# Two f32 products of raw tiles in the first block, and the first logit sum of four block pairs moved behind the up-weights

## The chip, the cores and the metric

The kernel runs on one core of one Trainium2 chip. The metric is the device time of one execution in microseconds (us). The core's engines each run their own instruction stream in order and wait for each other by semaphores: TensorE (PE, with its weight loads listed apart as PEld), VectorE (DVE), ScalarE (ACT), GpSimd (POOL) and SyncE (SP). In this kernel SP and POOL issue nearly all the transfers (DMAs).

## What is computed

```python
x = A_x                                              # 1 x 2048 x 640, f32
g = sigmoid((x * gate_w).sum(-1, keepdims=True))     # one gate for each of the 2048 positions
a = Re(DFT_seq(DFT_hidden(x)))                       # four f32 matrix products by cosine and sine tables
b = (gelu(x @ w_gate) * (x @ w_up)) @ w_down         # w_gate, w_up: 640 x 1728
return g * a + (1 - g) * b
```

All operands are f32. The sum `x * gate_w` that stands under the sigmoid is called the logit sum below; there are 16 of them, each for 128 positions.

## The kernel before

**Products in parts.** An f32 operand is split in a high part (ACT rounds it to the type fp32r, `high`, L82) and a low part (DVE subtracts the high part from the raw tile, `low`, L85). `mm3` (L101 to L103) makes a product of three fp32r matmuls: high by high, high by low, low by high. A matmul of a raw f32 tile without parts appears nowhere in this kernel.

**The first block.** The hidden width 1728 is 13 blocks of 128 and a rest of 64. The "mixed" block holds the 64 left columns of the gate and of the up matrix side by side; it is made first, along with gate block 0 and up block 0, in the banks `pm`, `pg` and `pu`, for the first two of four position tiles (512 positions each). The depth 640 is five steps `d` of 128. The part of the program from L1019 on is written out by hand in the order in which ACT, DVE and PE take it: PE first makes 14 matmuls of ones (`idle`, L1023) that need no load. Then step d = 0 of `pm` is made in two halves of 256 positions with three fp32r matmuls each (L1051), so that the first half can start when half of the x tile is there. `pg` and `pu` follow with `mm3` on all 512 columns, then the same three for the second position tile, `x012`. The raw tiles are `w0r` (weights) and `xr` (x), with `w0h`, `w0l`, `x011h`, `x011l` and so on as their parts. A number in a tile's name that is not part of the tile's own name is left out by the profile, so every raw x tile reads `xr`.

**The pairs of blocks.** Blocks 1 and 2 are made one by one, and the other ten in five pairs, f and f + 1, for f = 3, 5, 7, 9 and 11. A pair's first block makes seven extra products across position tiles for the gate (banks such as `pH5t`, `pZ5t`) and seven for the up matrix (`pH5u`, `pZ5u`). The latter need the up-weights' sums and differences: raw tile `wu5r`, four DVE instructions (L246 to L249, `across`), the high part `wu5h` on ACT and the low part `wu5l` on DVE. They also need parts of x sums that were stored earlier and are loaded again by POOL: `xu` (three loads, `load_across`, L1150), and `xq` for the gate.

**What sets the order.** `fills` is a queue of small pieces of DVE and ACT work with a cost each. While PE's products are written out, `fill` takes pieces from its head in step with the cost of the products, so that the order in `fills` is the order on DVE, with the PE-driven instructions in between. In pairs 5, 7, 9 and 11 (`kind == 1 and f > PAIRED`) two logit sums are put in: `load_z(2)` returns a load and a sum (L720, tile `xz`, DVE) twice. The first load goes out at once. The first sum `z1` and the second load stand in the middle of `fills` (`len(fills) // 2`), the second sum `z2` at its end, ahead of the next block's weights (`work`). When they are placed, `fills` holds nine pieces: four sums left over from the block before, the three pieces of the up-weights (`across`, `high_u`, `low_u`) and the two pieces of the down-weights' sums (L595 to L600, tiles `dr` and `da`, stored by SP as `wsd`).

**Buffers.** All tiles of 4 KB a partition share 46 slots (`slot`). A tile gets a slot when the program asks for it, and the first write to it waits for the last use of the tile that had the slot before. So the order in which tiles are asked for decides which instruction waits for which.

**POOL's transfers.** The hidden rows go to device memory through POOL (`hA`, `hT`, L404, 256 KB each), which issues them in order. A transfer of POOL waits for the transfer that was issued eight places before it, apart from its data.

Of the kernel before, what the change touches and what calls it, by code (L numbers as in the profile page):

```python
# [37 lines left out]
def kernel(  # L38
# [27 lines left out]
    nc = tc.nc  # L66
# [317 lines left out]
    def load_first():  # L384

        r, h, l = ([slot(dt, [P, 8, P], f"w0{n}{k}") for k in range(2)] for n, dt in (("r", F32), ("h", F32R), ("l", F32R)))
        W = {n: [tuple(v[c // 8][:, c % 8] for v in (h, l)) for c in range(k, 3 * ND, 3)] for k, n in enumerate("mgu")}

        def at8(v, a, b):
            return v[a // 8][:, a % 8 : a % 8 + b - a]  # L390

        def load(engine, a, b):
            engine.dma_start(at8(r, a, b), w0[:, a:b])

        def parts(do, a, b):
            if do is high:
                high(at8(h, a, b), at8(r, a, b))
            else:
                low(at8(h, a, b), at8(l, a, b), at8(r, a, b))

        return W, load, parts

    def keep(to, i, src):
        nc.gpsimd.dma_start(to[:, i], src)  # L404
# [580 lines left out]
            put(2 * q + 1, 0, a[q])  # L985


    W0, load_part, parts = load_first()
    Bs = []
    B, tiles, load, piece, tsum, his, lows = load_x(0)  # L990

# [4 lines left out]
    halves = [slice(0, T // 2), slice(T // 2, T)]  # L996
# [22 lines left out]
    with in_order(ACT, DVE, PE):  # L1019
        nc.scalar.activation(table, table, AF.Gelu_apprx_tanh)  # L1020
        idle = bank("idle")
        for k in range(14):
            nc.tensor.matmul(idle[:, halves[k % 2]], *ones, start=k == 0, stop=True, skip_group_check=True)  # L1023
        bk1, bk2 = first_banks(0, 1), first_banks(0, 2)
        for d in range(ND):
            raw, _, (h, l) = piece(d, 1)
            first, *rest = FIRST[d]
            parts(high, *first)
            if d == 0:
                a, b = halves  # L1030
                nc.vector.tensor_copy(h[:, a], raw[:, a])
                parts(low, *first)
                low(h[:, a], l[:, a], raw[:, a])
                split(h[:, b], l[:, b], raw[:, b])
                parts(high, *rest[0])
                parts(low, *rest[0])
            else:
                high(h, raw)
                parts(low, *first)
                low(h, l, raw)  # L1040
                for r in rest:
                    parts(high, *r)
                for r in rest:
                    parts(low, *r)
            split_piece(d, 2)
            if d == 0:
                wh, wl = W0["m"][0]
                for c in halves:
                    for k, (w, x) in enumerate(((wh, h), (wl, h), (wh, l))):
                        first = k == 0 and c is halves[0]  # L1050
                        nc.tensor.matmul(bk1["m"][:, c], w, x[:, c], start=first, stop=False, skip_group_check=True)  # L1051
                for n in "gu":
                    mm3(bk1[n], W0[n][0], (h, l), True, False)
            else:
                first_products(bk1, W0, B, 1, [d])
            first_products(bk2, W0, B, 2, [d])
# [121 lines left out]
    with in_order(PE, ACT, DVE, POOL):  # L1178
        for f in range(1, NF):
# [24 lines left out]
            if kind == 1 and f > PAIRED:  # L1204
                (_, first), z1, (_, second), z2 = load_z(2)
                first()
                k = len(fills) // 2
                more = list(fills)
                fills.clear()
                fills.extend([*more[:k], z1, (0, second), *more[k:], z2, *work])  # L1210
            elif f in ZE_AT:
                (_, first), z1 = load_z(1)
                first()
                fills.insert(5, z1)
# [45 lines left out]
            W = nxt  # L1260
# [438 lines left out]
```

## Time and profile before

| what | us |
|---|---|
| median of 3 runs (1020.52 to 1021.36) | 1020.55 |
| the profiled execution's own time | 1021.83 |
| its span, first to last instruction | 1020.0 |
| PE busy, 4483 matmuls | 1015.6 |
| DVE busy, 1154 instructions | 823.2 |
| ACT busy, 622 instructions | 486.1 |
| POOL busy | 166.9 |

The profiled execution took 1.8 us more than its span; a launch lies around the span. It took 1.3 us more than the median of the runs that were timed without a profile. Times of single events below are counted from the span's start. Matmuls overlap by a part of their length, so the distance between two starts, not their duration, is what one costs. A row of the timeline gives start, duration, engine, line, what is written from what, and in square brackets how long the engine sat idle before it and what released it.

### The profile page before, as it was taken

Reading aid. Unit: us, or ns where it says so; the run is one execution under the profiler, and the core shown is the slowest. Engines: PE = TensorE matmul, PEld = TensorE weight load, DVE = VectorE, ACT = ScalarE, POOL = GpSimd, SP = SyncE. Lnnn points to the kernel's source line nnn. Section 1 sums busy time; section 2 is a strip of 40 time slices with the busy share of each in tenths; the row PEclk is TensorE's granted clock in tenths of the full one; section 3 lists DMA queues with packets and bytes.
Section 4 is the critical chain, followed back from the end, with each engine's and each line's share of the span. In section 5 each row is a group of like instructions: output and inputs, shape, how many; then the busy total and the mean of one; then the engine's idle time right before and its main releaser. Section 6 shows DMA issues by size and latency. Waiting matters only on the chain.

```text
span 1020.0 us, 13269 instructions
## 1 busy us (share of the span) xinstructions
PE 1015.6 (100%) x4483; PEld 840.2 (82%) x4483; DVE 823.2 (81%) x1154; ACT 486.1 (48%) x622; POOL 166.9 (16%) x295
## 2 busy tenths in 40 slices
PE   9999999999999999999999999999999999999998
PEld 7888888888888888888888888888888888888887
DVE  6987877787787989888887976898588869797796
ACT  5544534353535667557444443444344444455440
POOL 0122242323231200100001012102210200021112
PEclk9999999999999999999999999999999999999999
DMA  7468588968699999979874669668866877897856
GB/s 271 168 209 276 181 264 275 314 225 290 201 315 313 415 374 383 330 245 329 295 254 172 213 223 337 223 200 298 302 203 209 294 252 275 295 349 215 274 134 99
DMA packets 96644, 267.58 MB, mean 262 GB/s; under 512 B 12672, under 2 KB 27008, under 8 KB 96576
## 3 DMA queue, kind: packets, MB, share of 16 engines
q1 hardware_dynamic: 70512, 185.24, 53.2%
q0 software_dynamic: 25776, 81.30, 24.4%
q8 instruction: 35, 0.57, 0.2%
q14 instruction: 33, 0.27, 0.1%
q10 hardware_dynamic: 288, 0.20, 0.1%
HBM read 192.48 MB, written 70.27 MB: 258 GB/s over the span
## 4 chain that ended last, share of the span: by engine, by line
PE 97%; issue 1%; DMA 1%; DVE 0%; POOL 0%; POOLq 0%
PE pX L103 6%; PE pX L102 6%; PE pX L101 6%; PE pZ L103 4%; PE pZ L102 4%; PE pZ L101 4%; PE pL L102 3%; PE pL L103 3%; PE pL L101 3%; PE pV L102 2%; PE pV L103 2%; PE pV L101 2%; PE pY L102 1%; PE pR L103 1%; PE pQ L101 1%; PE pQ L102 1%
## 5 line engine op out<-in xcount | busy, mean ns | idle before, releaser
L82 ACT ACTIVATE ch<-csa 128x1024 fp32r<-128x1024 f32 x32 | 34.0, 1063 | 78.2 <-DVE csa L770 76.7
L85 DVE TENSOR_TENSOR cl<-cra,ch 128x1024 fp32r<-128x1024 f32 x32 | 39.1, 1222 | 24.6 <-ACT ch L82 22.5
L82 ACT ACTIVATE ch<-cra 128x1024 fp32r<-128x1024 f32 x32 | 33.9, 1059 | 52.3 <-DVE cl L85 19.3
L85 DVE TENSOR_TENSOR cl<-crb,ch 128x1024 fp32r<-128x1024 f32 x32 | 39.1, 1223 | 14.4 <-ACT ch L82 14.4
L102 PE MATMUL pL<-cl,xah 128*128 128x512 f32 x128 | 49.9, 390 | 0.0
L103 PE MATMUL pL<-ch,xal 128*128 128x512 f32 x128 | 49.9, 390 | 0.0
L101 PE MATMUL pL<-ch,xah 128*128 128x512 f32 x128 | 49.7, 390 | 0.0
L82 ACT ACTIVATE ch<-crb 128x1024 fp32r<-128x1024 f32 x32 | 33.8, 1055 | 31.2 <-PE pL L102 11.4
L404 POOL DMA_DIRECT2D hA<-s x48 | 26.1, 544 | 132.7 <-DVE s L562 113.1
L85 DVE TENSOR_TENSOR cl<-csb,ch 128x1024 fp32r<-128x1024 f32 x32 | 39.2, 1225 | 3.7 <-ACT ch L82 2.3
L85 DVE TENSOR_TENSOR cl<-csa,ch 128x1024 fp32r<-128x1024 f32 x32 | 39.1, 1221 | 2.1 <-ACT ch L82 1.1
L82 ACT ACTIVATE ch<-csb 128x1024 fp32r<-128x1024 f32 x32 | 34.0, 1062 | 11.7 <-DVE csb L773 4.7
L556 ACT ACTIVATE s<-s 128x512 f32<-128x512 f32 x24 | 15.2, 633 | 46.7 <-DVE s L555 46.7
L148 ACT ACTIVATE s<-pX 128x512 f32<-128x512 f32 x40 | 23.5, 598 | 23.7 <-PE pX L103 22.4
L85 DVE TENSOR_TENSOR kl<-kw,kh 128x1024 fp32r<-128x1024 f32 x24 | 29.4, 1223 | 4.5 <-DMA kw<-in_wd 2.6
L82 ACT ACTIVATE kh<-kw 128x1024 fp32r<-128x1024 f32 x24 | 25.3, 1052 | 16.1 <-PE kR L103 6.2
L551 DVE TENSOR_TENSOR s<-s,pX 128x512 f32<-128x512 f32 x24 | 16.5, 686 | 19.6 <-PE pX L103 14.3
L1346 POOL DMA_DIRECT2D uA<-c x8 | 4.3, 542 | 168.9 <-DVE c L1448 168.7
L404 POOL DMA_DIRECT2D hT<-s x48 | 26.0, 541 | 24.3 <-DVE s L579 8.1
L929 POOL DMA_DIRECT2D out<-ks x12 | 6.5, 541 | 136.8 <-DVE ks L928 136.2
L101 PEld LDWEIGHTS pL<-ch,xah 128*128 128x128 f32 x128 | 24.0, 188 | 5.0
L102 PEld LDWEIGHTS pL<-cl,xah 128*128 128x128 f32 x128 | 24.0, 188 | 5.0
(3612 smaller groups left out, 3483.8 us busy)
## 6 DMA issues: line engine op xcount, KB each, us to landing
cra<-in_ct SPq DMA_DIRECT2D x64, 512.0 KB, 4.6
crb<-in_ct SPq DMA_DIRECT2D x64, 512.0 KB, 5.0
hA<-s POOLq DMA_DIRECT2D x48, 256.0 KB, 5.9
hT<-s POOLq DMA_DIRECT2D x48, 256.0 KB, 5.7
kr<-hA SPq DMA_DIRECT2D x24, 512.0 KB, 7.7
kr<-hT SPq DMA_DIRECT2D x24, 512.0 KB, 6.8
ux<-uA SPq DMA_DIRECT2D x24, 512.0 KB, 5.9
ux<-uT SPq DMA_DIRECT2D x16, 512.0 KB, 6.7
```

The source lines that it names most:

```text
L82: nc.scalar.activation(hi, raw, AF.Copy)
L85: nc.vector.tensor_tensor(lo, raw, hi.bitcast(F32), op=ALU.subtract)
L101: nc.tensor.matmul(ps, lh, rh, start=first, stop=False, skip_group_check=True)
L102: nc.tensor.matmul(ps, lh, rl, start=False, stop=False, skip_group_check=True)
L103: nc.tensor.matmul(ps, ll, rh, start=False, stop=last, skip_group_check=True)
L148: nc.scalar.activation(m, src, AF.Copy)
L404: nc.gpsimd.dma_start(to[:, i], src)
L551: tt(s5, s5, X, op=ALU.add)
L556: nc.scalar.activation(s2, s2, AF.Gelu_apprx_tanh)
L929: nc.gpsimd.dma_start(acc4[:, t] if tp and e == 4 else out[2 * tp + t, e], src)
L1346: nc.gpsimd.dma_start(to[:, i], src)
```

## The change

Three places differ.

```diff
@@ load_first
-        return W, load, parts
+        return W, r[0][:, 0], load, parts
@@ the first block
-    W0, load_part, parts = load_first()
+    W0, w0m, load_part, parts = load_first()
...
-        for k in range(14):
+        for k in range(12):
             nc.tensor.matmul(idle[:, halves[k % 2]], *ones, start=k == 0, stop=True, skip_group_check=True)
...
             if d == 0:
-                wh, wl = W0["m"][0]
                 for c in halves:
-                    for k, (w, x) in enumerate(((wh, h), (wl, h), (wh, l))):
-                        first = k == 0 and c is halves[0]
-                        nc.tensor.matmul(bk1["m"][:, c], w, x[:, c], start=first, stop=False, skip_group_check=True)
+                    first = c is halves[0]
+                    nc.tensor.matmul(bk1["m"][:, c], w0m, raw[:, c], start=first, stop=False, skip_group_check=True)
                 for n in "gu":
                     mm3(bk1[n], W0[n][0], (h, l), True, False)
@@ the pairs 5, 7, 9 and 11
                 (_, first), z1, (_, second), z2 = load_z(2)
                 first()
-                k = len(fills) // 2
+                k = len(fills) - 2
                 more = list(fills)
                 fills.clear()
                 fills.extend([*more[:k], z1, (0, second), *more[k:], z2, *work])
```

The first block's six fp32r matmuls of 256 columns become two f32 matmuls on the raw tiles, and the matmuls of ones go from 14 to 12. The parts of these tiles are still made, since `pg`, `pu` and the second position tile use them. In the pairs the first sum and the second load now stand behind seven of the nine pieces instead of four, that is behind the up-weights' `across`, `high_u` and `low_u`.

PE at the program's start, before. The `x011h` and `x011l` are parts of the first x tile, `w0h` and `w0l` of the first weights.

```order
L1023 MATMUL idle<-const-bfloat16-1.0 128x256
L1051 MATMUL pm_193<-x011h,w0h_138 128x256
L1051 MATMUL pm_193<-x011h,w0l_140 128x256
L1051 MATMUL pm_193<-x011l,w0h_138 128x256
L1051 MATMUL pm_193<-x011h,w0h_138 128x256
L1051 MATMUL pm_193<-x011h,w0l_140 128x256
L1051 MATMUL pm_193<-x011l,w0h_138 128x256
L101 MATMUL pg_194<-x011h,w0h_138 128x512
```

And in the changed kernel:

```order
L1023 MATMUL idle<-const-bfloat16-1.0 128x256
L1049 MATMUL pm_191<-xr_142,w0r_136 128x256 x2
L101 MATMUL pg_192<-x011h,w0h_138 128x512
L102 MATMUL pg_192<-x011l,w0h_138 128x512
L103 MATMUL pg_192<-x011h,w0l_140 128x512
```

The two raw products read the loaded tiles themselves and wait for their loads alone; the first instruction that waits for DVE's and ACT's parts is now `pg`'s.

DVE in pair 5, before. L720 is a logit sum (two instructions), L246 to L249 and `wu5l` belong to the up-weights, L454 to L460 read PE's banks, and L595 to L600 are the down-weights' sums.

```order
L720 ISA xz_1411,z<-xz_1411,gwb 128x640
L720 ISA z 128x1
L454 TENSOR_TENSOR s_1431<-s_1431,pH5t 128x512
L246 TENSOR_TENSOR wu5r<-wu5r 128x128
L247 TENSOR_TENSOR wu5r<-wu5r 128x128
L248 TENSOR_TENSOR wu5r<-wu5r 128x128
L249 TENSOR_TENSOR wu5r<-wu5r 128x128
L459 TENSOR_TENSOR s_1450<-s_1450,pZ5t 128x512
L460 TENSOR_TENSOR s_1450<-s_1450,pX_1_1461 128x512
L85 TENSOR_TENSOR wu5l<-wu5r,wu5h 128x640
L595 TENSOR_TENSOR dr_1407<-da_1408,dr_1407 128x256
```

And in the changed kernel:

```order
L246 TENSOR_TENSOR wu5r<-wu5r 128x128
L247 TENSOR_TENSOR wu5r<-wu5r 128x128
L248 TENSOR_TENSOR wu5r<-wu5r 128x128
L249 TENSOR_TENSOR wu5r<-wu5r 128x128
L454 TENSOR_TENSOR s_1425<-s_1425,pH5t 128x512
L459 TENSOR_TENSOR s_1444<-s_1444,pZ5t 128x512
L460 TENSOR_TENSOR s_1444<-s_1444,pX_1_1455 128x512
L85 TENSOR_TENSOR wu5l<-wu5r,wu5h 128x640
L720 ISA xz_1405,z<-xz_1405,gwb 128x640
L720 ISA z 128x1
L595 TENSOR_TENSOR dr_1401<-da_1402,dr_1401 128x256
```

The sum moved past eight instructions and stands between the low part and the down-weights' sums; pairs 7, 9 and 11 read the same.

SP in pair 5, with the semaphores that each row waits for: the two `xz` loads and the first store of the down-weights' sums. Before:

```order
L716 DMA xz_1411<-in_xz 128x640 [waits DMASW4_49,DMASW6_49,DVE_49,DMAHW4_49,PE_49,Activation_49]
L716 DMA xz_1482<-in_xz 128x640 [waits DMASW7_49,DMASW5_49,DMAHW5_49,PE_49,Activation_49]
L602 DMA wsd_128<-dr_1407 128x256 [waits DMAHW6_49,DMAHW3_49,DVE_49]
```

And in the changed kernel:

```order
L716 DMA xz_1405<-in_xz 128x640 [waits DMASW4_49,DMASW6_49,DVE_49,DMAHW4_49,PE_49,Activation_49]
L716 DMA xz_1507<-in_xz 128x640 [waits DMAHW2_49,DMAHW5_49,DMAHW1_49,DVE_49]
L602 DMA wsd_128<-dr_1401 128x256 [waits DMAHW6_49,DMAHW3_49,DVE_49]
```

SP's order is the same, but the slots changed hands. The second `xz` now gets the slot of the raw up-weights `wu5r`, so its load waits for their last reader, DVE's `wu5l` (L85). On POOL the second `xu` load had that slot; it now gets the slot of the first `xz` and waits for DVE's first logit sum instead of DVE's `wu5l`. In pairs 7 and 9 the same two waits change. In pair 11 the second `xz` gets the slot of a hidden tile and waits for POOL's `hT` stores of it, and it is the third `xu` load that waits for `wu11l`.

## The prediction

> **What bounds the kernel now.** I read the page's head first, then PE's waits by its weight loads, then the timeline at the start and in the pairs.
>
> ```profile
> span 1020.0 us, 13269 instructions
> PE 1015.6 (100%) x4483; PEld 840.2 (82%) x4483; DVE 823.2 (81%) x1154; ACT 486.1 (48%) x622; POOL 166.9 (16%) x295
> PEld pH7u L101 <- DMA xu<-xv: 0.5, 1, 0.5
> PEld pm L102 <- DVE x012l L85: 0.4, 1, 0.4
> PEld pm L1051 <- ACT w0h L82: 0.2, 1, 0.2
> PEld pH7t L101 <- DVE s L454: 0.2, 1, 0.2
> ```
>
> PE is busy for 1015.6 of 1020.0 us. The last four rows (what waited, for what: total, times, longest) are all the waits of its weight loads, 1.3 us beside 0.8 us at the launch. Two lie in the first block and two in pair 7, so the edits touch all that there is. They cannot shorten the stream of products behind them. What they can win is at most these 1.3 us; what they can lose is open.
>
> **The first block.** The timeline of the start:
>
> ```profile
> 0.78 3.14 PE L1023 MATMUL idle<-const-bfloat16-1.0 128*128 128x256 bf16 x14 [0.78 <-PEq L1687]
> 3.33 0.31 ACT L82 ACTIVATE w0h<-w0r 128x128 fp32r<-128x128 f32 x1 [0.17 <-DMA w0r<-in_w]
> 3.69 0.58 PE L1051 MATMUL pm<-x011h,w0h 128*128 128x256 f32 x1
> 3.74 0.42 ACT L82 ACTIVATE x011h<-xr 128x256 fp32r<-128x256 f32 x1
> 4.55 0.42 DVE L85 TENSOR_TENSOR w0l<-w0r,w0h 128x256 fp32r<-128x256 f32 x1
> 4.95 0.41 PE L1051 MATMUL pm<-x011h,w0l 128*128 128x256 f32 x1
> 5.16 0.42 PE L1051 MATMUL pm<-x011l,w0h 128*128 128x256 f32 x1
> 5.37 0.63 PE L101 MATMUL pg<-x011h,w0h 128*128 128x512 f32 x1
> 5.80 0.63 PE L102 MATMUL pg<-x011l,w0h 128*128 128x512 f32 x1
> 6.23 0.63 ACT L82 ACTIVATE x012h<-xr 128x512 fp32r<-128x512 f32 x1 [1.76 <-DMA xr<-in_xt]
> 6.89 0.69 DVE L85 TENSOR_TENSOR x012l<-xr,x012h 128x512 fp32r<-128x512 f32 x1 [1.93 <-ACT x012h L82]
> 7.24 0.40 PE L101 MATMUL pm<-x012h,w0h 128*128 128x512 f32 x1
> 7.64 0.51 PE L102 MATMUL pm<-x012l,w0h 128*128 128x512 f32 x1
> ```
>
> Removed: six products from 3.69 to 5.37, that is 1.68 us, which wait for parts on the way. Added: two raw products. They need the loads alone, which ACT's row puts at 3.3 for the weights; the second half of x is there by 3.74, where ACT reads it. The twelve matmuls of ones end two steps of 3.14/14 = 0.22 us sooner, at about 3.5, so PE goes over without a gap that matters. The parts made on DVE and ACT stay, and the last that `pg` needs, `w0l`, ends at 4.97.
>
> No f32 product of raw tiles stands in this trace. Below, a pass over 256 columns costs 0.21 us here (4.95 to 5.16), and a raw product is at least one; above, it is unlikely to cost more than twice what three parts cost on PE without waits, 2 x 0.64 = 1.3 us. Nearest is the work itself: high by high, high by low and low by high in one instruction, and the product of the low parts, so four passes, 0.86 us. I take 0.86: the pair then runs from 3.4 to 5.1, and `pg` starts 0.25 us sooner.
>
> The Trainium skill says the same count: "FP8 and Floating Point Precision", section "TensorE Precision Notes", gives four passes for true FP32. By it the exchange is a loss of PE work, eight passes for six, and pays only by the waits that it removes; no run here shows it yet.
>
> What is late next decides: `pm` of the second tile needs `x012l`, which ends at 7.58 after a load that arrives at 6.23, and the edit moves neither. PE reached that point 0.17 us early already (7.24 and a step of 0.23 make 7.47 against 7.64). So 0.25 us more of lead becomes 0.25 us more of waiting: **worth 0.0 us**. With one pass each it is still 0.0. With 1.3 us each the pair ends at 6.0, 0.63 late; six products and a bit at 0.43 us before 6.3 and 0.23 after pass on about half of that, 0.33, less the lead of 0.17: +0.2.
>
> **The pairs.** DVE in pair 5 first, then the second sum with what follows, SP, POOL and ACT there:
>
> ```profile
> 150.19 0.69 DVE L585 TENSOR_TENSOR s<-s,s 128x512 f32<-128x512 f32 x1
> 153.50 0.83 DVE L720 CUSTOM_DVE_ANT_0 xz<-xz,gwb 128x640 f32<-128x640 f32 x1 [2.62 <-DMA hA<-s]
> 154.25 0.68 DVE L454 TENSOR_TENSOR s<-s,pH5t 128x512 f32<-128x512 f32 x1
> 156.50 0.69 DVE L460 TENSOR_TENSOR s<-s,pX 128x512 f32<-128x512 f32 x1
> 158.22 0.82 DVE L85 TENSOR_TENSOR wu5l<-wu5r,wu5h 128x640 fp32r<-128x640 f32 x1 [1.04 <-DMA hT<-s]
> 160.68 0.82 DVE L720 CUSTOM_DVE_ANT_0 xz<-xz,gwb 128x640 f32<-128x640 f32 x1
> 162.10 0.29 DVE L309 TENSOR_TENSOR wa6r<-wa6r 128x128 f32<-128x128 f32 x1
> 144.76 3.05 SPq L716 DMA_DIRECT2D xz<-in_xz  x2
> 159.45 1.13 POOL L1150 DMA_DIRECT2D xu<-xv  x2 [4.31 <-DVE dr L595]
> 162.42 0.63 ACT L82 ACTIVATE wa<-wa6r 128x512 fp32r<-128x512 f32 x1
> 165.88 0.60 ACT L148 ACTIVATE s<-pH5u 128x512 f32<-128x512 f32 x1 [1.34 <-PE pH5u L103]
> ```
>
> The first sum waits 2.62 us, with the up-weights queued behind it. Behind it they start at 150.9, and L460 ends 2.6 + 0.75 us sooner. But `wu5l` itself waits until 158.2 for an `hT` store that frees its slot, so this gain ends in a longer wait there: cover, not time. Then the sum stands in front of L595, and DVE is 0.75 us later from there (153.50 to 154.25 is its cost), the second `xu` load with it, which now waits for this sum.
>
> Against that stands the DMA. Shares of 16 engines in two stretches, and the transfers of `xz` and `xu`:
>
> ```profile
> 150.00:155.30 5.30, 5.30 (x25) 4.41 (x24) 2.68 (x8) 0.00 (x0) 2.18 (x4) 1.00 1.03 417
> 155.30:160.00 4.70, 4.70 (x23) 3.88 (x22) 3.52 (x9) 1.92 (x4) 0.55 (x1) 1.00 0.76 279
> xz<-in_xz SPq DMA_DIRECT2D x10, 320.0 KB, 7.8
> DMA to landing us min/median/max: 3.0/7.8/9.6
> L101 PE MATMUL pH5u<-xu,wu5h x2: 389/390/390, 165.0 to 167.0; 128*128 128x512 f32 x2
> DMA to landing us min/median/max: 5.2/5.6/6.1
> ```
>
> The engines are full (1.03, 417 GB/s) while the `hT` stores queue, and the second `xz`, 320 KB, leaves this stretch for one at 0.76. At 417 GB/s that is 0.8 us of transfer, so the stores and with them `wu5l` come up to 0.8 us sooner, and none at all if the eight-deep order of POOL's issues sets them. I take 0.6, nearer the full engines.
>
> The second `xu` of pair 5: issue 159.45 + 0.75 - 0.6 = 159.6, landing 5.2 later at 164.8, PE takes it at 165.0: **0.0**. Without relief 165.4: +0.4.
>
> The second `xz` now leaves SP after `wu5l`, at 159.0 - 0.6 = 158.5. Its sum stood at 160.68 and with the first sum ahead cannot start before 160.8. Queued behind it on DVE is L309, behind that on ACT the part of `wa6r` and the copies of `pZ5u`, `pV5u` and `pH5u`; PE waits for the last. ACT idles 1.34 us before that copy, and the copy ends (166.48) 0.5 before PE's use at 167.0. So the sum may start until 160.68 + 1.34 + 0.5 = 162.5, four us after the load's issue. The ten loads took 3.0 to 9.6; the long ones were issued into the full stretch. I take 3.5, near the minimum, since the front's loads have landed by then: **0.0**.
>
> The Trainium skill ("DMA: Bandwidth & Descriptors", section "Queues, rings and completion order") has each engine take turns between queues by packets, so that this load shares with POOL's `xu` and does not stand behind it; by that a time near the minimum is likely, but no row here shows it.
>
> Pair 7 is the tightest:
>
> ```profile
> 202.20 0.83 DVE L720 CUSTOM_DVE_ANT_0 xz<-xz,gwb 128x640 f32<-128x640 f32 x1 [3.64 <-DMA hT<-s]
> 206.46 0.82 DVE L85 TENSOR_TENSOR wu7l<-wu7r,wu7h 128x640 fp32r<-128x640 f32 x1 [0.57 <-DMA hT<-s]
> 207.69 5.28 DMA xu<-xv
> 213.00 0.19 PEld L101 LDWEIGHTS pH7u<-xu,wu7h 128*128 128x128 f32 x1 [0.54 <-DMA xu<-xv]
> ```
>
> The wait of 3.64 us held up L454, for which PE waited 0.2; that goes, and PE is at `pH7u` 0.2 sooner. But there it waits for `xu` as before, which lands at 212.96 + 0.75 - 0.6 = 213.1: **+0.15 us** in all. Without relief +0.75, with 0.8 us of it -0.05. In pairs 9 and 11 no wait of PE is listed and I cost them at nothing: the same `xu` lead covers 0.15.
>
> **Sum.** 0.0 (start) + 0.0 (pair 5) + 0.15 (pair 7) = +0.15 us on the profiled span of 1020.0, so 1020.15. That execution took 1021.83 and the median of the runs is 1020.55, 1.3 us less; to the median I add the same difference: **1020.7 us**.
>
> **Rivals.** First, the second `xz` lands late. From 4 us after its issue each us of delay is a us of PE's in pair 5, by way of L309 and ACT's copies, and likewise in pair 7 (its sum is at 208.91). With 5.0 us, the time of a load that shares all the way (an `xu` takes 5.2), it is +1.0 in each, 1022.7; with the median of 7.8 +3.8 in each, 1028. For it: the median of ten; against it: the load moves out of the full stretch. Slower, chance 0.22.
>
> Second, more relief than I take: if the stores land 1.3 us sooner, `xu` of pair 7 arrives before PE (213.1 - 0.7 = 212.4, where PE now stands), both its waits go, and the time is 1020.55 - 0.7 = 1019.8. For it: all four pairs lose a load from the full stretch; against it: 320 KB at 417 GB/s are 0.8 us only. Chance 0.14.
>
> Third, PE's rate at the start. Steps of 512 columns go from 0.43 us (5.37 to 5.80) to 0.23 after 6.3. If the raw products or the two matmuls fewer put this off by one us, the us costs 0.5; by three, 1.5 less the lead of 0.17: 1021.9.
>
> The Trainium skill ("TensorE: Matmul & The Clock Gate", section "Part 1: The HAM clock gate") has the rate follow PE's activity in free-running windows of 3.4 us; here PE stays occupied from 0.78 on, so by it nothing shifts.
>
> Against the third rival: two steps are 0.4 us, and the raw products fill them. Chance 0.06.
>
> Fourth, the edit at the start does win: if the second position tile were ready sooner, 0.25 us would count as 0.1 to 0.2: 1020.4, inside my range; nothing in the diff moves that load.
>
> **How the numbers follow.** No change worth telling, 1020.7: chance 0.58, its own range 1020.2 to 1021.6 (all relief to none in both pairs: -0.05 to +0.4 + 0.75 - 0.15). The range reaches to the second rival below and to a landing of 5 us in two pairs above: 1019.7 to 1023. A measurement of this kernel tells 0.2%, 2.0 us, from no change. Faster than 1018.5 is more than all the waits together: 0.02. Slower than 1022.6 is most of the first rival and a rest: 0.20. Within: 0.78.
>
> **What would show it.** At the start, raw products some 0.86 us apart, `pg` near 5.1, and the product with `x012l` still near 7.64. In the pairs, no idle time of DVE ahead of L246 and a longer one ahead of `wu5l`, `wu5l` some 0.6 us sooner, and the second `xz` landing within 4 us. It would be wrong if DVE idles over 1.5 us before the second sum and ACT's copy of `pH5u` comes behind PE's need, or if PE's wait at `pH7u` goes away.

## The result, and the profile after

| | us |
|---|---|
| before, median of 22 runs (1020.52 to 1022.94) | 1021.25 |
| changed, median of 22 runs (1020.94 to 1026.02) | 1023.18 |
| ratio, 95% interval | 1.0017 (1.0011 to 1.0023) |
| profiled execution of before: span, its time | 1020.0, 1021.83 |
| profiled execution of the change: span, its time | 1021.7, 1023.5 |

The medians differ by 1.9 us; the ratio is 1.0017. That is within the 0.2% that the forecast called no change, but it is not the 0.15 us of its sum, and the time lies 0.2 us above the upper end of the range. The changed kernel also spreads more: 5.1 us between its runs, 2.4 between those of before.

The head of the page after, and all waits of PE's weight loads for a `xu` load or in the first block (what waited, for what: total, times, longest):

```profile
span 1021.7 us, 13258 instructions
PEld pH7u L101 <- DMA xu<-xv: 1.5, 1, 1.5
PEld pH5u L101 <- DMA xu<-xv: 1.1, 1, 1.1
PEld pm L102 <- DVE x012l L85: 0.5, 1, 0.5
PEld pm L1049 <- DMA xr<-in_xt: 0.5, 1, 0.5
PEld pm L101 <- ACT x012h L82: 0.4, 1, 0.4
PEld pm L1049 <- DMA w0r<-in_w: 0.3, 1, 0.3
PEld pg L101 <- ACT w0h L82: 0.3, 1, 0.3
```

Before, the one wait for `xu` was 0.5 us in pair 7. Now pair 5 waits 1.1 and pair 7 1.5. Three stretches, each about one pair, show how much of the span this is: the columns are the stretch, its length, then the busy time of PE, PEld, DVE, ACT and POOL, the granted clock, the DMA share and GB/s. Before:

```profile
143.00:190.00 47.00, 47.00 (x209) 38.87 (x208) 37.18 (x73) 21.25 (x35) 13.80 (x24) 1.00 0.88 282
191.00:239.00 48.00, 47.88 (x212) 39.16 (x211) 35.92 (x70) 21.40 (x36) 13.74 (x24) 1.00 0.78 260
239.00:287.00 48.00, 48.00 (x213) 39.72 (x212) 35.72 (x70) 21.79 (x36) 13.77 (x24) 1.00 0.78 256
```

and after:

```profile
143.00:190.00 47.00, 46.27 (x205) 37.92 (x203) 36.70 (x72) 20.88 (x35) 13.80 (x24) 1.00 0.88 275
191.00:239.00 48.00, 46.92 (x207) 38.48 (x206) 35.52 (x70) 21.25 (x35) 13.74 (x24) 1.00 0.78 256
239.00:287.00 48.00, 48.00 (x213) 39.67 (x213) 35.34 (x68) 22.17 (x36) 13.76 (x24) 1.00 0.79 252
```

PE works 0.73 us less in the first stretch and 0.96 less in the second; the sum, 1.69, is the difference of the spans (1020.0 and 1021.7). So the loss is in pairs 5 and 7, at `pH5u` and `pH7u`. The timeline of pair 5 after (DVE, SP, POOL):

```profile
156.69 0.82 DVE L85 TENSOR_TENSOR wu5l<-wu5r,wu5h 128x640 fp32r<-128x640 f32 x1 [3.24 <-DMA hT<-s]
157.43 0.82 DVE L720 CUSTOM_DVE_ANT_0 xz<-xz,gwb 128x640 f32<-128x640 f32 x1
157.54 0.33 SPq L716 DMA_DIRECT2D xz<-in_xz  x1
158.66 1.13 POOL L1148 DMA_DIRECT2D xu<-xv  x2 [4.62 <-DVE dr L595]
160.57 0.82 DVE L720 CUSTOM_DVE_ANT_0 xz<-xz,gwb 128x640 f32<-128x640 f32 x1 [0.59 <-DMA xz<-in_xz]
```

and its chain of waits:

```profile
158.66 6.90 DMA xu<-xv
165.57 0.04 issue
165.61 0.50 PE pH5u L101
```

`wu5l` starts at 156.69, where it was 158.22 before: the front of the pair is relieved by more than was taken. The sum stands between `wu5l` and the second `xu` load as the order has it. But the second `xz` load leaves SP at 157.54, and from 158.66 on the `xu` loads run beside it; the second `xu` load takes 6.90 us where 5.2 was kept. PE stands ready at 164.7 and gets it at 165.61. The second `xz` itself lands 3.0 us after its issue, so that DVE idles 0.59 us ahead of the second sum and ACT is not late.

It helps to count every pair from the start of its first product (`pH5t` and so on). If nothing is late, PE reaches the product with the second `xu` load 21.84 us later and the next pair 47.68 us later: both numbers return to within 0.02 us in every profile of this study wherever nothing is late. The landing of the second `xu` load is then a sum of three terms, all in us:

| pair 5 | low part of wu starts | to the xu issue | xu to landing | sum | need |
|---|---|---|---|---|---|
| before | 15.06 | 1.23 | 5.17 | 21.46 | 21.84 |
| as forecast | 14.46 | 1.98 | 5.2 | 21.6 | 21.84 |
| changed | 13.81 | 1.97 | 6.90 | 22.7 | 21.84 |
| **pair 7** | | | | | |
| before | 15.61 | 1.23 | 5.28 | 22.1 | 21.84 |
| as forecast | 15.01 | 1.98 | 5.28 | 22.3 | 21.84 |
| changed | 14.40 | 1.98 | 6.66 | 23.0 | 21.84 |

The relief is 1.2 us in both pairs where 0.6 was taken, the sum's term is 0.75 as taken, and the transfer, which was taken as unchanged, is 1.4 to 1.7 us longer.

The start, PE's rows of the timeline:

```profile
3.29 1.90 PE L1049 MATMUL pm<-xr,w0r 128*128 128x256 f32 x4
5.00 0.50 PE L101 MATMUL pg<-x011h,w0h 128*128 128x512 f32 x1
7.39 0.50 PE L102 MATMUL pm<-x012l,w0h 128*128 128x512 f32 x1 [0.23 <-DVE x012l L85]
```

and its weight loads:

```profile
3.29 0.50 PEld L1049 LDWEIGHTS pm<-xr,w0r 128*128 128x128 f32 x2 [0.27 <-DMA w0r<-in_w]
4.24 0.50 PEld L1049 LDWEIGHTS pm<-xr,w0r 128*128 128x128 f32 x2 [0.46 <-DMA xr<-in_xt]
5.00 0.19 PEld L101 LDWEIGHTS pg<-x011h,w0h 128*128 128x128 f32 x1 [0.25 <-ACT w0h L82]
```

The two raw products take 1.71 us together, from 3.29 to 5.00 (3.4 to 5.1 was forecast), though PE's rate may have risen before their end. The 0.46 us that the second weight load waits for the second half of x cost PE nothing: the four matmul records of the first row have no idle time between them, as PE still works on the first product at 4.24. The weight loads then wait 0.4 us for `x012h` and 0.5 for `x012l`, where they waited 0.4 for `x012l` alone before. The product with `x012l` starts at 7.39 and not at 7.64 because the load of that x tile landed 0.25 us sooner (ACT reads it at 5.98 after 6.23 before). In the fourteen profiles of this study `x012l` ends between 6.51 and 7.58, with and without the first block's edit.

### The profile page after: what moved, and what is told of

Its sections match the earlier page's. It is cut to its first block, busy times and chain, and to the rows that moved or that the text cites. A ratio compares the mean times of both kernels' runs of the same rounds, so it can differ in the third digit from the quotient of the medians.

```text
span 1021.7 us, 13258 instructions
## 1 busy us (share of the span) xinstructions
PE 1015.3 (99%) x4479; PEld 838.6 (82%) x4479; DVE 823.4 (81%) x1154; ACT 487.4 (48%) x622; POOL 166.9 (16%) x295
## 4 chain that ended last, share of the span: by engine, by line
PE 94%; DMA 2%; issue 2%; DVE 1%; POOL 1%; SPq 0%; ACT 0%; POOLq 0%
PE pX L103 6%; PE pX L101 6%; PE pX L102 6%; PE pZ L103 4%; PE pZ L101 4%; PE pZ L102 4%; PE pL L102 3%; PE pL L103 3%; PE pL L101 3%; PE pV L102 2%; PE pV L103 2%; PE pV L101 2%; PE pY L102 1%; PE pR L102 1%; PE pQ L102 1%
## 5 line engine op out<-in xcount | busy, mean ns | idle before, releaser
L85 DVE TENSOR_TENSOR cl<-cra,ch 128x1024 fp32r<-128x1024 f32 x32 | 39.1, 1222 | 26.8 <-ACT ch L82 24.6
L85 DVE TENSOR_TENSOR cl<-crb,ch 128x1024 fp32r<-128x1024 f32 x32 | 39.1, 1222 | 14.1 <-ACT ch L82 14.0
L85 DVE TENSOR_TENSOR cl<-csb,ch 128x1024 fp32r<-128x1024 f32 x32 | 39.2, 1224 | 3.7 <-ACT ch L82 2.3
L85 DVE TENSOR_TENSOR cl<-csa,ch 128x1024 fp32r<-128x1024 f32 x32 | 39.1, 1221 | 2.1 <-ACT ch L82 1.1
L85 DVE TENSOR_TENSOR kl<-kw,kh 128x1024 fp32r<-128x1024 f32 x24 | 29.3, 1220 | 3.7 <-DMA kw<-in_wd 2.6
L537 ACT ACTIVATE s<-pZ 128x512 f32<-128x512 f32 x24 | 13.9, 594 | 38.3 <-PE pZ L103 22.0
```

What stands on the lines that cost most here:

```text
L85: nc.vector.tensor_tensor(lo, raw, hi.bitcast(F32), op=ALU.subtract)
L537: nc.scalar.activation(s5, Z, AF.Copy)
```

## The experiments

Two theories that share all but one term. **S**: the second `xz` load, now beside the second `xu` load, lengthens it. **D**: the moved sum's 0.75 us in front of that load is the cost. Two rivals: **B**, the first block costs; **C**, the second sum comes late and holds up ACT. The expectations of the first four runs call S "A". The runs were made in three groups, each with its own runs of before: median 1021.11 beside the first four, 1021.02 beside load_quarter, sum_quarter, sum_in_gap and after_again, 1020.84 beside the rest; every ratio is against the runs of before in its group. Each median is over 10 or 11 runs, that of load_early and of sum_in_gap over five. "Lost" is what the three distances between the starts of pairs 5, 7, 9 and 11 exceed 47.68 us by, in the profiled execution.

| kernel | median, us | ratio (95%) | second xu load, pairs 5, 7, 9, 11 | lost, us |
|---|---|---|---|---|
| before (profile above) | | | 5.17, 5.28, 5.15, 5.22 | 0.45 |
| changed (profile above) | 1023.18 | 1.0017 (1.0011 to 1.0023) | 6.90, 6.66, 5.57, 6.52 | 2.40 |
| start_only | 1021.13 | 0.9999 (0.9990 to 1.0008) | 4.86, 4.96, 6.09, 5.20 | 0 |
| pairs_only | 1022.50 | 1.0013 (1.0004 to 1.0022) | 5.28, 6.45, 6.43, 6.31 | 1.81 |
| load_early | 1024.43 | 1.0032 (1.0019 to 1.0044) | 5.05, 4.93, 5.33, 5.30 | 3.07 |
| sum_early | 1023.38 | 1.0018 (1.0009 to 1.0027) | 4.92, 6.64, 6.61, 5.69 | 3.20 |
| load_quarter | 1021.07 | 0.9999 (0.9990 to 1.0008) | 4.71, 4.82, 5.36, 5.69 | 0 |
| sum_quarter | 1022.97 | 1.0018 (1.0009 to 1.0027) | 6.97, 7.27, 7.58, 6.97 | 2.98 |
| sum_in_gap | 1029.33 | 1.0079 (1.0067 to 1.0092) | 4.93, 5.41, 5.52, 4.44 | 8.62 |
| after_again | 1023.48 | 1.0021 (1.0012 to 1.0029) | 5.61, 6.58, 5.46, 6.69 | 0.53 |
| both_quarter | 1020.78 | 0.9998 (0.9989 to 1.0007) | 4.73, 4.74, 5.32, 5.59 | 0 |
| load_half | 1020.88 | 1.0000 (0.9991 to 1.0009) | 4.69, 4.70, 4.86, 5.73 | 0 |
| pairs_again | 1023.79 | 1.0029 (1.0020 to 1.0038) | 5.88, 5.51, 7.65, 6.42 | 2.57 |
| one_sum | 1020.83 | 0.9999 (0.9991 to 1.0008) | 6.16, 6.68, 6.88, 5.60 | 0 |

### Which half of the diff

**start_only** is the changed kernel with the pairs as before:

```
-                k = len(fills) - 2
+                k = len(fills) // 2
```

> Only the first block's edit: two raw f32 products and 12 matmuls of ones; the pairs as before. Theory A (the pairs lose the time, by the second xz load that now shares the DMA engines with the xu loads): this part is worth 0 to -0.5 us against the kernel before, and PE's only waits in the pairs are those of before (0.5 us at pH7u for xu, 0.2 for L454). Theory B (the first block costs something that the profile of one execution hides): slower than before by 1 us or more. In both the product with x012l starts within 0.3 us of the end of x012l.

1021.13 against 1021.11, and nothing lost in the pairs. The first block's edit is worth nothing that these runs can tell (0.1% either way), as forecast, and B's loss of 1 us or more falls.

**pairs_only** is the kernel before with only that line changed, from `len(fills) // 2` to `len(fills) - 2`.

> Only the pairs' edit: first logit sum and second xz load behind the up-weights, the first block as before. Theory A: all of the loss, +1.5 to +2.5 us against the kernel before, with PE waiting about 1 us at pH5u and 1.5 us at pH7u for xu, and nowhere for ACT's copies. Theory B: 0 to +1 us. Theory C (the second sum comes late and holds up ACT): PE waits for ACT's copies (L148) instead of xu.

1022.50, 1.4 us slower: the loss is the pairs'. In this profile PE waits for `xu` at `pH7u` (1.3 us) and `pH9u` (0.7), not at `pH5u`: which pair is late differs from execution to execution.

### The sum and the load apart

**load_early** (pairs only) moves the sum and leaves the second load at its old place. The two tiles are kept in a list, since both are loaded before either is summed:

```
-                k = len(fills) // 2
+                k, m = len(fills) // 2, len(fills) - 2
-                fills.extend([*more[:k], z1, (0, second), *more[k:], z2, *work])
+                fills.extend([*more[:k], (0, second), *more[k:m], z1, *more[m:], z2, *work])
```

> Pairs' edit with the second xz load left at its old place and only the first sum moved behind the up-weights; the second xu load still waits for that sum. No relief of the DMA engines in front, no new sharing behind. Theory A, sharing is most of it: the xu loads take 5.2 to 5.5 us as before, pH5u waits 0.4 us, pH7u about 1.3 us (0.5 + 0.75), +0.4 to +1.2 us against before. Theory D (the moved sum alone, by its 0.75 us in front of the xu load, makes the loss): as much as pairs_only, +1.7 us or more.

It is slower than the whole move, 1.0032, and S's expectation of 0.4 to 1.2 us is missed; D's, 1.7 or more, is met. PE's waits:

```profile
PEld pH5u L101 <- DMA xu<-xv: 1.2, 1, 1.2
PEld pH9u L101 <- DMA xu<-xv: 1.1, 1, 1.1
PEld pH7u L101 <- DMA xu<-xv: 0.9, 1, 0.9
```

Yet the second `xu` load takes 4.9 to 5.3 us, as before: with no second `xz` beside it there is no lengthening. What is late here is its issue: the low part of wu starts 16.03 us into pair 5, and the sum puts 1.98 behind it, so the landing is at 16.03 + 1.98 + 5.05 = 23.06. By the same sum, the moved sum behind the low part of before, without relief, would land at 15.06 + 1.98 + 5.17 = 22.2, 0.4 us late. The rest is this kernel's own: its slots change hands, and it is ACT's high part of the up-weights that waits for the `hT` stores there. So D has a part in this kernel's loss, and S is not the only price.

**sum_early** is the other half: the sum stays in the old place, the second load goes late (`k` and `m` as in load_early; only the last line is shown).

```
+                fills.extend([*more[:k], z1, *more[k:m], (0, second), *more[m:], z2, *work])
```

> The other half: the first sum stays in front of the up-weights, only the second xz load is asked for behind them; the second xu load waits for wu5l as before. In its new place the load goes out within 1 us of the xu load. Theory A: xu takes 6 us or more, pH5u waits 0.5 to 1.2 us and pH7u over 1 us, +0.7 to +1.5 us against before. Theory D: within 0.3 us of before, xu at 5.2 us.

1.0018, 2.3 us slower, where S had expected 0.7 to 1.5 and D nothing. PE's waits:

```profile
PEld pH9u L101 <- ACT s L148: 1.4, 1, 1.4
PEld pH5t L101 <- DVE s L454: 1.3, 1, 1.3
PEld pH7u L101 <- DMA xu<-xv: 0.8, 1, 0.8
```

Three ways to be late in one profile. In pair 7 the second `xu` load is issued only 1.22 us behind wu's low part but takes 6.64: S. In pair 9 the second `xz` lands 6.4 us after its issue, DVE idles 5.26 us in front of its sum, and ACT's copy comes late: C, the prediction's first rival, at work. In pair 5 the first sum waits 4.72 us and holds up L454. So either half alone costs about as much as both together: the move of the load gives relief and sharing, the move of the sum gives 0.75 us of delay and lets L454 go early.

For the transfer itself the two halves tell S from D. In before, start_only and load_early no second `xz` load goes out near the second `xu` load: eleven of their twelve take 4.86 to 5.33 us, one (start_only, pair 9) 6.09, the median is 5.2. In the change, pairs_only and their repeats below the whole `xz` load goes out about 1 us ahead of it: the sixteen take 5.28 to 7.65 us, the median is 6.4. The third `xu` load follows 0.6 or 0.7 us behind the second in all of these, and in load_early the moved sum stands ahead of it as in the change.

### Taking the sharing away, or the sum

**load_quarter** (pairs only) loads and sums 160 of the 640 columns in each pair's second logit sum; z is incomplete there:

```
-            nc.sync.dma_start(r[0][1], xz[sb])
+            nc.sync.dma_start(r[0][2][:, :c], xz[sb][:, :c])
-            nc.vector.tensor_tensor_reduce(v, v, gwb, 1.0, 0.0, ALU.mult, ALU.add, z[:, sb : sb + 1])
+            v = v[:, :c]
+            nc.vector.tensor_tensor_reduce(v, v, gwb[:, :c], 1.0, 0.0, ALU.mult, ALU.add, z[:, sb : sb + 1])
```

(Left out here: the line that sets `c` to 160 for the second of two loads and to 640 for all others, and the move of the sum as in pairs_only.)

> Only the pairs' edit, but each pair's second logit load, and its sum, take 160 of the 640 columns (80 KB for 320 KB; the rest of these four sums is left out). The first sum stands behind the up-weights' parts as in the change, 0.75 us in front of the second xu load. Theory S (the second xz load beside xu is what lengthens xu): the second xu load takes 5.0 to 5.6 us from issue to landing in pairs 5, 7 and 9 in place of 5.3 to 6.9; it is still issued 1.97 us behind the start of wu's low part; TensorE's waits for xu in the pairs sum to at most 0.5 us; median 1021.1 (0.6 either way). Rival D (the sum's 0.75 us in front of xu is what costs): waits stay at 1 us or more and the median at 1022 to 1023.

1021.07: the loss is gone, with the moved sum still between wu's low part and the `xu` issue (1.98 us in pair 5). **sum_quarter** is the counterpart: both loads whole, the first sum of each pair on 160 columns.

> Only the pairs' edit, but each pair's first sum, the moved one, works on 160 of the 640 columns (the rest of it is left out); both loads are whole. Theory S: the second xu load is issued about 1.4 us behind the start of wu's low part (1.97 with the whole sum), and still takes 6.2 to 6.9 us in at least two of the pairs 5, 7, 9, so that waits for xu of 0.3 to 1.0 us in all are left; median 1021.8 (0.6 either way). Rival D: no wait for xu is left and the median is before's, 1021.1.

1022.97, as slow as the change and slower than the 1021.8 that S had expected. PE's waits:

```profile
PEld pH5u L101 <- DMA xu<-xv: 1.3, 1, 1.3
PEld pH7u L101 <- DMA xu<-xv: 1.3, 1, 1.3
PEld pH9u L101 <- DMA xu<-xv: 0.7, 1, 0.7
PEld pH11u L101 <- DMA xu<-xv: 0.7, 1, 0.7
```

The second `xu` load is issued 0.5 us sooner (1.47 us behind wu's low part) and takes 7.0 to 7.6 us, longer in every pair than in the change: the half us won at the issue is spent beside the `xz` load. A sooner issue bought nothing here, so D alone is not the cause.

That the short load takes the loss away is not by itself proof of S in pairs 5, 7 and 9, since something else changed with it: slots changed hands again, and the third `xu` load goes out 2.2 to 2.4 us behind the second in load_quarter, where before and in the change it follows by 0.6. What moved on POOL's and on SP's queue while the second `xu` load of pair 5 (0.52 MB) was under way:

| pair 5 | second xu load, us | POOL's queue, MB | SP's queue, MB |
|---|---|---|---|
| before | 5.17 | 0.78 | 0.29 |
| load_early | 5.05 | 0.76 | 0.29 |
| changed | 6.90 | 1.02 | 0.89 |
| load_quarter | 4.71 | 0.53 | 0.56 |

In the change SP's queue moves three times as much beside the `xu` load as before; in load_early, with the sum moved and the load not, it moves what it did before. In load_quarter it still moves twice that, but POOL's queue moves little else than the `xu` load itself. So the time of load_quarter shows that the sum's 0.75 us can stand there without a loss; whether the fewer bytes of `xz` or the later third `xu` load made room for it is not shown.

**load_half** has 320 columns in the second load, else as load_quarter.

> Only the pairs' edit, with the second logit load and sum on 320 of 640 columns (160 KB; the rest of these four sums is left out). Theory S: between the short load (1021.07, no wait for xu in pairs 5, 7, 9) and the whole one (1022.5): the second xu load takes 5.0 to 6.2 us, waits for xu of 0.2 to 1.0 us in all, median 1021.6 (0.5 either way). If it is not bytes but the one more transfer that counts: as with the whole load, 1022.2 to 1023.

1020.88: no loss either, below the expected 1021.6. The two runs with short loads are not a clean dose in pairs 5, 7 and 9, since the slots changed hands once more. POOL's rows of the timeline in load_half:

```profile
158.53 0.55 POOL L1152 DMA_DIRECT2D xu<-xv  x1 [4.71 <-DVE dr L595]
160.89 0.54 POOL L1152 DMA_DIRECT2D xu<-xv  x1 [1.81 <-ACT s L148]
```

The third `xu` load leaves POOL 2.4 us behind the second, where before and in the change it is 0.6 us behind; so the second shares less with that one too. Pair 11 has not this fault: there the third follows by 0.6 or 0.7 us in all of them. For the second `xu` load of pair 11 alone, from issue to landing: start_only, with no `xz` load beside it,

```profile
DMA to landing us min/median/max: 5.2/5.2/5.2
```

load_half, with 160 KB beside it,

```profile
DMA to landing us min/median/max: 5.7/5.7/5.7
```

the change, with 320 KB beside it,

```profile
DMA to landing us min/median/max: 6.5/6.5/6.5
```

and sum_quarter, which also has 320 KB beside it:

```profile
DMA to landing us min/median/max: 7.0/7.0/7.0
```

The transfer is longer with the load beside it: 5.2 or 5.3 us without it (before, start_only, load_early), 5.6 to 5.7 with 80 or 160 KB (load_quarter, both_quarter, load_half), and 6.3 to 7.0 over the five profiles in which the whole load goes out 0.7 to 1.0 us ahead. In sum_early, where the whole load goes out 3.9 us ahead, it is 5.7. That is S in a place where the order of the `xu` loads is the same; SP's other transfers are not quite the same there (in before and start_only loads of `ua` run beside it), so the size is not that of the `xz` load alone.

**both_quarter** is the whole change with the short second load.

> The whole change, both parts, with each pair's second logit load and sum on 160 of 640 columns (the rest of these four sums is left out). If the sharing of the second load with xu is all that costs and the first block's edit is worth nothing in either setting: 1021.0 (0.5 either way), ratio 0.9992 to 1.0006, as with the pairs' edit alone and the short load (1021.07). Rival B (the first block's edit costs once the pairs are changed, which is why the whole change stands at 1.0017 to 1.0021 and the pairs alone at 1.0013): 1021.6 or more.

1020.78, ratio 0.9998: with the short second load both parts of the change are free, as expected, and B falls here too. The third `xu` load is late in pairs 5, 7 and 9 of this kernel as well (2.2 to 3.8 us behind the second).

### Other places for the sum

**sum_in_gap** is the change with the first sum one place earlier, into the 3.2 us that DVE idles ahead of `wu5l`:

```
-                k = len(fills) - 2
+                k = len(fills) - 3
```

> The whole change, with the first sum one place earlier: ahead of wu's low part, where VectorE idles over 3 us for a store, and not behind it; the second load follows the sum. Both theories: the second xu load is issued about 1.2 us behind the start of wu's low part (0.75 earlier than in the change), the second xz load leaves SP some 2.5 us earlier and lands before the second xu load is issued, so xu takes 5.0 to 5.5 us; no wait of TensorE for xu over 0.3 us in any pair; median 1020.7 (1019.9 to 1021.3), 0.4 faster than before. Rival R (the earlier second load crosses the hT stores and takes the relief back): wu's low part starts 1 us or more later than in the change (157.9 or later in pair 5), waits of 0.5 to 1.0 us for xu come back, and the median is 1021.5 to 1022.5.

The worst of all, 1029.33, and wrong by both theories. DVE's, SP's and ACT's rows of the timeline in pair 5:

```profile
152.99 0.82 DVE L720 CUSTOM_DVE_ANT_0 xz<-xz,gwb 128x640 f32<-128x640 f32 x1
153.92 0.83 DVE L85 TENSOR_TENSOR wu5l<-wu5r,wu5h 128x640 fp32r<-128x640 f32 x1
157.10 0.33 SPq L716 DMA_DIRECT2D xz<-in_xz  x1
164.28 0.83 DVE L720 CUSTOM_DVE_ANT_0 xz<-xz,gwb 128x640 f32<-128x640 f32 x1 [7.82 <-DMA xz<-in_xz]
166.03 0.63 ACT L82 ACTIVATE wa<-wa6r 128x512 fp32r<-128x512 f32 x1 [4.46 <-DVE wa6r L309]
168.04 0.60 ACT L148 ACTIVATE s<-pH5u 128x512 f32<-128x512 f32 x1
```

and PE's waits:

```profile
PEld pH7u L101 <- ACT s L148: 3.3, 1, 3.3
PEld pH5u L101 <- ACT s L148: 2.6, 1, 2.6
```

The wait for the `hT` stores has not gone; it belongs to a slot, and the slot has gone from `wu5l` to the second `xz` load. `wu5l` now runs at 153.9 and the second `xu` load lands at 160.1, 4.3 us ahead of PE. But the `xz` load waits until 157.10, shares with the `xu` loads and takes 7.0 us, and its sum, with L309 and ACT's copies queued behind it, is 4 us late. This is the chain of the prediction's first rival, step by step: DVE's idle time, L309, ACT's `wa`, the copy of `pH5u`.

The waits explain only part of the loss: they are 2.6 and 3.3 us, but pairs 5 and 7 are 4.1 and 4.6 us longer. Behind each of the two waits the granted clock is 0.50 for 3.4 us (169.6 to 173.0 and 220.8 to 224.2), and a product of 512 columns takes 0.43 us there in place of 0.23. No other profile shows this after its start and ahead of its last 4 us; the longest wait of PE's weight loads in the pairs of the others is 1.5 us.

**one_sum** keeps that place and gives each pair one load and sum only; the four others go to the blocks of f = 4 and 10 and to two more steps of the down stage:

```
-                (_, first), z1, (_, second), z2 = load_z(2)
+                (_, first), z1 = load_z(1)
-                k = len(fills) - 2
+                k = len(fills) - 3
-                fills.extend([*more[:k], z1, (0, second), *more[k:], z2, *work])
+                fills.extend([*more[:k], z1, *more[k:], *work])
-ZB_AT = [5,7,9,14,15,16]
-ZE_AT = [6, 8]
+ZB_AT = [5,7,8,9,10,14,15,16]
+ZE_AT = [4, 6, 8, 10]
```

> The first block's edit as in the change; each pair has only one logit load and sum, in VectorE's idle place ahead of wu's low part, and the four second ones go to the blocks of f = 4 and 10 and to two more steps of the down stage. All 16 sums are made. Theory S: wu's low part starts no later than in the change, the second xu load is issued about 1.2 us behind it and takes 4.7 to 5.4 us, TensorE waits for xu in no pair; median 1020.6 (0.6 either way), at or a little under the kernel before. Rival: the four loads collide elsewhere (the blocks of f = 4 and 10, the down stage) and give back 1 us or more, 1022 to 1023.

No wait for `xu` is listed and nothing is lost in the pairs, at 1020.83 against 1020.84 before. Its second `xu` loads take 5.6 to 6.9 us with no `xz` load beside them (4.7 to 5.4 was expected), but in pairs 5, 7 and 9 they are issued some four us sooner, since they wait for the early sum and not for wu's low part (the expected 1.2 us behind it is missed on the good side), and land at 160.5 in pair 5, four us ahead of PE. It does not beat the kernel before. The reason is seen in the others that lose nothing: start_only, load_quarter, load_half and both_quarter stand at 1020.8 to 1021.1 too. The 0.5 and 0.2 us of waits in the profile of before were probably not there in its median execution, of which there is no profile: the profiled one has a span of 1020.0, the runs of before next to the median of 1020.84 one of 1019.0, which is one_sum's span, and start_only, with the pairs of before, has a span of 1018.8 without any wait in the pairs.

### Repeats

**after_again** and **pairs_again** are the changed kernel and pairs_only once more.

> The change itself beside the three others on one chip. Every theory: 1.001 to 1.0025 of the kernel before, with TensorE's waits for xu in pairs 5, 7 and 9 summing to 1.5 to 3 us.

> The pairs' edit alone, once more, for the question whether the first block's edit adds to it: if not, pairs alone is as slow as the whole change, ratio 1.0015 to 1.0022 (1022.6 to 1023.3); if it does, 1.0008 to 1.0014 again. Second xu load 6 us or more in at least two of pairs 5, 7, 9, 11.

1.0021, as expected, and 1.0029, above what either answer had expected. The first time the pairs alone looked cheaper (1.0013) than the whole; the second time dearer. The intervals of the whole change overlap both, so nothing says that the first block adds or saves anything. The profiled execution of after_again is one of the quickest of its kernel, span 1019.5, and waits 0.6 us for `xu` at `pH7u` and 0.3 at `pH11u` (1.5 to 3 us in pairs 5 to 9 was expected); in pairs_again PE waits for `xu` in three pairs:

```profile
PEld pH9u L101 <- DMA xu<-xv: 1.5, 1, 1.5
PEld pH7u L101 <- DMA xu<-xv: 0.8, 1, 0.8
PEld pH5u L101 <- DMA xu<-xv: 0.6, 1, 0.6
```

Its second `xu` loads take 5.5 to 7.7 us. This spread is that of the times: 1020.59 to 1025.55 for after_again, 1020.18 to 1021.58 for both_quarter.

## Why the prediction was partly right

- **The bound and the ceiling.** Right. PE's stream did not get shorter, and none of the eleven changed kernels has a median more than 0.1 us under that of before beside it. The ceiling of 1.3 us was too high: it was read from one execution that had 0.7 us of waits in pair 7, and the kernels without any such wait are no faster than before in the median.
- **The first block, worth 0.0.** Right, by start_only, and by both_quarter beside load_quarter. The wait moved to `x012h` and `x012l` as said. The price of a raw product was right too: in one_sum, where PE keeps the rate of the start for all of it, the matmul records start at 3.87, 4.29 and 4.72, 0.43 us apart, and a product has two of them, so 0.86 us. PE's rate did not rise later than before (the third rival): 512 columns take 0.23 us from 5.34 on after and from 6.54 on before. By the granted clock the rise comes between 3.5 and 6.4 us in the fourteen profiles, with and without this edit.
- **The first sum's wait of 2.62 us ends in a longer wait ahead of `wu5l`.** Right: 3.24 us, for an `hT` store.
- **The sum's 0.75 us in front of the second `xu` load.** Right to 0.01 us in both pairs.
- **The relief, 0.6 us.** Too small: 1.2 in both pairs of the two profiles. Other executions have a start of wu's low part at 13.6 to 14.8 us in pairs 5 and 7 with the pairs' edit and at 14.65 and 15.25 in start_only, so part of the 1.2 is the difference of one execution from another. The issue on POOL and the transfer both came sooner: the last `hT` store that `wu5l` waits for went out 9.28 us into pair 5 before and 8.69 after, and took 5.71 and 5.04 us. The order of POOL's issues that was set against the relief is one place shorter than stated ahead of the prediction: no POOL transfer here goes out before the one seven places ahead of it has landed, 22 of before's go out 0.31 us behind that landing, and none of before's comes closer than 1.15 us to the landing eight places ahead. The second rival's relief (1.3) was nearly there, but its end was not: PE's wait at `pH7u` grew.
- **The second `xz`, landing within 4 us.** Right in pairs 5 and 7 (3.0), slightly over in 9 and 11 (4.3 and 4.2), and DVE idled 4.87 us before the second sum in pair 11 without ACT becoming late for PE. The first rival did not come about in the change. That it is real is shown by sum_early and sum_in_gap, where PE waited 1.4 us once, and 2.6 and 3.3.
- **The step that failed: "issue 159.45 + 0.75 - 0.6 = 159.6, landing 5.2 later at 164.8".** The prediction said of the second `xz` that it leaves SP at 158.5 and takes 3.5 us, so until 162.0, and issued the `xu` loads into the middle of that, at 159.6. It asked what the `xu` loads do to `xz`, and gave that a rival; it did not ask what `xz` does to the `xu` load on which PE waits. The `xu` term is 6.90 and 6.66 us, not 5.2: +1.7 and +1.4 where +0.0 stood. With that term and its own relief the sum would have been 14.46 + 1.98 + 6.9 = 23.3 in pair 5, 1.5 us late, and the forecast slower. That the `xz` load lengthens this term is shown by the profiles with and without it (median 6.4 and 5.2 us, load_early among the latter) and by pair 11; that the sum's 0.75 us in front is not the loss by itself is shown by sum_quarter, which loses as much with 0.5 us of it taken away. Pairs 9 and 11, costed at nothing, lost nothing in the change's profile, but pair 9 waited 0.7 and 1.5 us for `xu` in pairs_only and pairs_again. That the measured time lies so near the upper end of the range is luck: that end was set by the first rival, which did not come about.
- **The Trainium skill's rule on sharing** ("DMA: Bandwidth & Descriptors", "Queues, rings and completion order": each engine takes turns between its queues). It was cited for a short time of `xz`, and the change's trace agrees with that (3.0 us in pairs 5 and 7). The same rule read from the other queue's side says that `xu` gets longer, which is what the trace shows (5.2 to 6.9 us in pair 5).
- **The base.** The forecast was hung on a median of three runs, 1020.55; over 22 runs it is 1021.25. That is 0.7 of the 2.5 us between 1020.7 and 1023.18. The statement that the profiled execution ran 1.3 us above the median comes from the same three runs. The lower end of the forecast's own range does not follow from its bracket either: 1020.55 - 0.05 is 1020.5, not 1020.2.

What stays open: why the transfer takes 5.3 us in one execution and 7.6 in another with the same order of issues, and so how much each pair loses on average. Whether the missing loss of load_quarter, load_half and both_quarter in pairs 5 to 9 is due to fewer bytes of `xz` beside the `xu` load or to the third `xu` load's later issue was not told apart.

## What to carry to other kernels

When a load is moved out of a crowded stretch, list what is in flight where it lands, and lengthen the transfer on which the bound engine waits there, not only the moved one: here a 512 KB load with 320 KB issued about 1 us ahead of it took 6.4 us where it took 5.2 (medians), though in single executions hardly more than before (5.28) or 2.5 us more (7.65), and PE's new waits in the change were waits for that load. A wait for a slot goes to whoever gets the slot: after a reorder read again what each load and each first write waits for, since an instruction that was moved into an idle place may hand the wait on to something less patient. And a wait in one profiled execution is a ceiling for that execution only; kernels with none of them in the pairs ran no faster in the median.

## What was not expected of the hardware

- An f32 product of raw tiles (128x128 by 256 columns) leaves two weight loads and two matmul records. At the rate of the start its records stand 0.43 us apart (one_sum), so 0.86 us a product, four times the 0.21 us of one pass of a product in parts at the same rate (before). In start_only, where PE's rate rises inside the two products, the records stand 0.22 and 0.21 us apart.
- The time of one and the same load in one and the same place varies by up to two us between executions when another queue's load runs beside it (pair 9: 5.46 to 7.65 us in the four profiles of the change and of pairs_only). Without that neighbour the four of before stay within 0.13 us of each other, but those of start_only, with the same order, go from 4.86 to 6.09.
- After PE had stood idle for over 2 us in sum_in_gap, its granted clock was 0.50 for 3.4 us (both times), so a wait of 2.6 us cost 4.1.
